# Another written order for the attention steps, the loads and the first expert's steps of an attention and mixture-of-experts kernel

## Chip, cores and metric

The kernel runs on one core of a Trainium2 chip. The metric is the device time of one execution in microseconds (us). The kernel before takes 1009.96 us, the median of three runs (1009.75 to 1012.1).

## What is computed

Two layers follow each other. The first is linear attention with exponential features, for 8 batches of 8 heads, 576 tokens and 64 values per head. The second takes its output as 4608 rows of 512 values and sends every row through all 8 experts, weighted by a routing matrix that eight rounds of row and column normalization make.

```
proj = einsum('bhsd,df->bhsf', x, w_phi)            # x is q or k
proj = proj - max(abs(proj), axis=-1)
phi  = concatenate([exp(proj), exp(-proj)], axis=-1)
kv = einsum('bhsf,bhsd->bhfd', phi_k, v);  z = sum(phi_k, axis=2)
attn = einsum('bhsf,bhfd->bhsd', phi_q, kv) / (einsum('bhsf,bhf->bhs', phi_q, z) + 1e-6)
...
P = exp(logits)                                     # logits = x @ w_gate
for _ in range(8): P /= P.sum(1); P /= P.sum(0); P *= N / E
for e in range(8): out += P[:, e:e+1] * (maximum(x @ w1[e], 0) @ w2[e])
```

## The kernel before, in words

**Records and planner.** The kernel's Python code does not issue instructions at once. Each operation is recorded with its engine, a cost in microseconds, the buffers and keys that it reads and writes, and a rank, which is its place in the recorded sequence (`Plan.op`). A scheduler (`Plan.schedule`) then walks through a modelled time: of all operations whose inputs are there and whose buffers can be had, it takes the one that can start first, and among equals the one recorded first. The instructions are written to each engine's queue in that order, and on the chip each engine works through its queue in order. So the recorded sequence is a priority, and the planner's costs decide the rest. Buffers are rings: an operation that needs a slot waits until an earlier user has given it back.

**The order string.** For the attention, its loads and the first expert, the recorded sequence is a string of 322 letters, `order` in line 1102 and after. Each letter records the next step of its kind. With head pairs counted j = 0 to 31 (batch j // 4, two heads each):

- `l` (14): loads the Q, K and V of half a batch (four heads). For batches 0 and 1 Q and K go through SyncE's queue (SP) in float32. From batch 2 on they go through GpSimd's queue (POOL, line 550) and are cast to bf16 on the way. V goes through SP (line 558).
- `e` (4): loads the 64 last tokens of each head, the "rests", of one or two batches (lines 600 to 607).
- `w` (8): loads a quarter of the first expert's w1 (the first four, line 527) or w2 (line 531), through POOL.
- `t` (12): from batch 2 on, a DMA transpose of a half batch's Q and K, issued by SP (line 567). There are two buffers of loaded Q and K (`qk`), and three of transposed ones (`qkT`).
- `r` (8): the features of a batch's rests (line 678 transposes, line 727 a small GpSimd step, lines 732 and 737 V scaled by GpSimd into `vrd`).
- `a` (32): a pair's K side. For batches 0 and 1 TensorE transposes Q and K (line 752) and VectorE and ScalarE copy them (lines 756, 760). Then come four K projections on TensorE (256 columns each), maxima on VectorE (line 614), exponentials on ScalarE (line 618), a sign change by GpSimd (line 808), the exponentials of the maxima `em`, and V scaled with them by GpSimd (lines 810 and 816).
- `q` (32): the four Q projections and their maxima. `p` (32): the Q features, two 512-column matmuls and four exponentials.
- `b` (32): the KV product of a pair, 18 small matmuls, and its copy by VectorE (line 892).
- `n`, `m` (32 each): the outputs of the pair's first and second head (line 905 on TensorE, lines 913, 918 and 919 on VectorE).
- `c` (32): the pair's output transposed into `xT`, by TensorE (line 934) and VectorE (line 937) in batches 0, 1, 2 and 7, by a DMA transpose (line 928) in batches 3 to 6.
- `g` (8): a batch's rests transposed (line 944), and its routing logits.
- `u` (24), `d` (20): up-projection (eight 512-column matmuls, `ps<-xT,w` under line 622) and down-projection (the same size, `ps<-w,hx`) of the first expert, for a quarter of a 512-token group. A `u` needs that group's `xT` and w1, a `d` the group's four `u` and w2.

Most matmuls of these steps are recorded by one helper and stand under line 622.

**Loads wait for the order too.** A load step carries `gates()`: it waits for the maxima of the last `q` and the last `a` that stand before it in the string. So a letter's place moves the load itself, not only its rank.

**After the string.** The rest of the first expert fills the time of the routing rounds, and then the other seven experts follow with a two-level fast multiplication, each with an order of its own written out. None of that changes.

Of the kernel before, what the change touches and what calls it, by code (L numbers as in the profile page):

```python
# [349 lines left out]
def kernel(  # L350
# [739 lines left out]
    def stage_g(b):  # L1090
# [9 lines left out]
             "c": lambda j: pair_c(j // 4, j % 4, xbs[j]), "g": stage_g,  # L1100
             "u": lambda i: up0(i // 4, i % 4), "d": lambda i: down0(i // 4, i % 4)}
    order = (
        "lraeaepqbwlqaqawwabwmqlltnrbppnwqbppmrmanbqaqmwwacmpnpbccpwbtcnmqnaqbclupunm"
        "taumquglcapalbcpnqqdcenmucugbblnapmrcqdutabnqpmunpbambccddnqplanmqmducpblttb"
        "augnaqlnrbdcampcadmqeutunqcppmdcaqtdqabpbbmlrqtdnpmuaqualbnagnacctbmqulupran"
        "tdpmtdqcmdnpdabdancpcabbqmpumqbcdgnappqunburqcbugmmnqdcdanumupqbnucmcpnmbddp"
        "bqmpncncubncmmgccg"
    )
    for i, n in enumerate(order):
        at[0] = i  # L1110
# [948 lines left out]
```

## Time and profile before

| quantity | value |
|---|---|
| median of the runs | 1009.96 us (1009.75 to 1012.1) |
| profiled execution, first to last instruction | 1008.8 us |
| TensorE busy (PE) | 994.0 us, 8376 matmuls |
| VectorE busy (DVE) | 898.6 us |
| ScalarE busy (ACT) | 812.8 us |
| GpSimd busy (POOL) | 447.6 us |
| attention on TensorE | until about 205 us, mixed with the first expert |
| granted TensorE clock | 1.000 |

The profile is of one execution. A row of the timeline gives the start and the length of an instruction (or of several alike in a row) in microseconds, then engine, line, operation, output tile, input tiles and shape; a bracket names the idle time ahead of it and who ended it. A matmul's row shows its whole passage: a stream of 512-column matmuls of 379 ns each starts a new one every 215 ns or so, so the step from start to start is what one costs. `SPq` and `POOLq` rows are the issuing of DMAs, not their transfer. A table of stretches gives each engine's busy time between two times.

### The profile page before, as it was taken

The numbers are of one execution on the slowest core, as the hardware profiler recorded it, in microseconds if no ns is written. First come the engines' busy times: TensorE is split into PE (matmuls) and PEld (weight loads), VectorE is DVE, ScalarE is ACT, GpSimd is POOL, SyncE is SP. The second block draws the span as 40 slices with busy tenths as digits, with TensorE's granted clock in tenths as the row PEclk, the third lists the DMA queues.
The fourth block names the chain that finished last, engine by engine and source line by source line (L and its number), as shares of the span: only waits on it lengthen the run. The fifth ranks groups of instructions, "written<-read, shape, count | busy, mean of one in ns | idle before, by whom it ended". The sixth has DMA issues, their size and how long they took to land.

```text
span 1008.8 us, 23309 instructions
## 1 busy us (share of the span) xinstructions
PE 994.0 (99%) x8376; PEld 727.7 (72%) x8376; DVE 898.6 (89%) x1999; ACT 812.8 (81%) x1930; POOL 447.6 (44%) x514
## 2 busy tenths in 40 slices
PE   7899999999999999999999999999999999999998
PEld 5666666644566877777777877787778777787775
DVE  7999998987888998899989898989889988989886
ACT  7999999845979788878878788777887888778874
POOL 5778674400133344434444444444443444344443
PEclk9999999999999999999999999999999999999999
DMA  9999999181136423282327133632246222724653
GB/s 249 183 202 183 157 153 144 38 170 56 53 121 143 147 97 98 84 184 96 109 98 170 44 100 131 130 127 98 97 117 177 97 98 84 147 79 142 208 174 126
DMA packets 129748, 128.86 MB, mean 128 GB/s; under 512 B 55776, under 2 KB 98272, under 8 KB 129632
## 3 DMA queue, kind: packets, MB, share of 16 engines
q1 hardware_dynamic: 97680, 103.33, 36.3%
q0 software_dynamic: 31648, 23.86, 16.9%
q8 instruction: 65, 1.06, 0.5%
q14 instruction: 51, 0.42, 0.2%
q10 hardware_dynamic: 304, 0.20, 0.1%
HBM read 122.50 MB, written 19.53 MB: 141 GB/s over the span
## 4 chain that ended last, share of the span: by engine, by line
PE 92%; DVE 3%; ACT 2%; DMA 2%; issue 1%; POOL 0%; DVEq 0%
PE ps L1466 41%; PE ps L1475 20%; PE ps L622 17%; PE ps L1607 11%; PE ps L905 2%; DMA xi6t<-X 1%; DMA xi<-X 1%; PE ps L752 1%; ACT q L618 0%; DVE m L614 0%; ACT k L618 0%; DVE wx L614 0%; DVE X L1240 0%; DMA acc<-in_k_dram 0%; DVE hs L1676 0%
## 5 line engine op out<-in xcount | busy, mean ns | idle before, releaser
L1875 POOL TENSOR_TENSOR acc<-acc,hx 128x512 f32<-128x512 f32 x186 | 236.1, 1276 | 404.7 <-ACT hx L1872 135.0
L1466 PEld LDWEIGHTS <-hs 128*128 128x128 bf16 x1984 | 194.1, 98 | 46.4 <-issue 0.2
L1872 ACT ACTIVATE hx<-ps,P 128x256 f32<-128x256 f32 x372 | 158.9, 483 | 53.4 <-PE ps L1466 52.0
L1860 DVE SCALAR_TENSOR_TENSOR acc<-ps,P,acc 128x256 f32<-128x256 f32 x372 | 162.2, 478 | 30.2 <-PE ps L1466 28.2
L1475 PE MATMUL ps<-xT,T 128*128 128x512 bf16 x608 | 171.0, 379 | 0.0
L1466 PEld LDWEIGHTS <-hx 128*128 128x128 bf16 x1488 | 145.6, 98 | 24.9
L1466 PE MATMUL ps<-hx,hs 128*128 128x256 bf16 x992 | 144.3, 273 | 0.0
L1676 DVE CUSTOM_DVE_ANT_0 hs<-ps,U 128x512 bf16<-128x512 f32 x192 | 124.7, 684 | 11.3 <-PE ps L1475 6.6
L1607 PE MATMUL ps<-xT 128*128 128x256 bf16 x576 | 125.4, 272 | 0.0
L1475 PEld LDWEIGHTS <-T 128*128 128x128 bf16 x672 | 65.8, 98 | 40.6
L1682 ACT ACTIVATE hs<-ps 128x512 bf16<-128x512 f32 x96 | 55.9, 598 | 41.7 <-PE ps L1475 40.2
L1466 PE MATMUL ps<-wx,hs 128*128 128x256 bf16 x560 | 78.4, 273 | 0.0
L622 PE MATMUL ps<-w,hx 128*128 128x512 bf16 x288 | 73.0, 379 | 0.0
L622 PE MATMUL ps<-xT,w 128*128 128x512 bf16 x288 | 72.9, 379 | 0.0
L1466 PE MATMUL ps<-wx,hx 128*128 128x256 bf16 x496 | 72.3, 273 | 0.0
L1676 DVE CUSTOM_DVE_ANT_0 hs<-ps,X 128x512 bf16<-128x512 f32 x96 | 65.1, 684 | 7.8 <-PE ps L1607 6.9
L1466 PE MATMUL ps<-hx 128*128 128x256 bf16 x496 | 71.2, 273 | 0.0
L1607 PEld LDWEIGHTS <-xT 128*128 128x128 bf16 x576 | 56.3, 98 | 17.5
L1466 PE MATMUL ps<-w,hx 128*128 128x256 bf16 x432 | 62.2, 273 | 0.0
L614 DVE TENSOR_REDUCE m<-ps 128x4 f32<-128x512 f32 x88 | 58.8, 680 | 3.7 <-PE ps L622 1.9
L1672 ACT COPY X<-ps 128x512 f32<-128x512 f32 x96 | 58.6, 610 | 2.5 <-DVE ps L1650 2.5
L1466 PE MATMUL ps<-w,hs 128*128 128x256 bf16 x432 | 60.2, 273 | 0.0
(174 smaller groups left out, 2256.0 us busy)
## 6 DMA issues: line engine op xcount, KB each, us to landing
xT<-xi SPq DMA_DIRECT2D x48, 448.0 KB, 4.6
xT<-xd SPq DMA_DIRECT2D x72, 256.0 KB, 4.0
wx<-in_moe_w_dram POOLq DMA_DIRECT2D x8, 1024.0 KB, 11.2
v_m<-in_v_dram SPq DMA_DIRECT2D x15, 512.0 KB, 5.2
out_dram<-acc SPq DMA_DIRECT2D x14, 512.0 KB, 3.0
w<-in_moe_w_dram POOLq DMA_DIRECT2D x6, 1024.0 KB, 11.0
xT<-xp SPq DMA_DIRECT2D x24, 256.0 KB, 2.8
qk<-in_k_dram POOLq DMA_DIRECT2D x12, 256.0 KB, 5.4
```

The costliest lines, as they stand in the source:

```text
L614: dve(el, lambda: nc.vector.tensor_reduce(out=dst(), in_=src(), axis=AX.X, op=ALU.max, apply_absolute_value=True), r, w)
L622: nc.tensor.matmul(out_, lhsT=lhsT, rhs=rhs, start=start, stop=stop)
L905: pe(65, lambda j=j: nc.tensor.matmul(pn()[:, j * D1:j * D1 + D1], lhsT=s["T"][x]()[:, j % 2, 2 * h + j // 2, :] if j < 4 else r["T"][x]() ...
L1466: pe(256, lambda i=i, k=k, z=z: nc.tensor.matmul(bank()[:, 256 * i:256 * i + 256], lhsT=lhs(k, i), rhs=rhs(k), start=first and z, stop=k = ...
L1475: pe(512, lambda k=k: nc.tensor.matmul(bank().rearrange("p (a b) -> p a b", a=2), lhsT=lhs(k), rhs=rhs(k), start=first and k == 0, stop=k ...
L1607: pe(256, lambda: nc.tensor.matmul(halves_of(bank[q], n)(), lhsT=lhs(), rhs=t()[:, rhs, :], start=start, stop=True, skip_group_check=True) ...
L1672: act(512, lambda: nc.scalar.copy(out=flat(to[q])(), in_=bank[q]()), [bank[q]], [(to[q], 0), (to[q], 1)])
L1676: dve(515, lambda: nc.vector._custom_dve(ADD_SAT, out=out_(q, i, j), in0=bank[q]().rearrange("p (a b) -> p a b", a=2), in1=to[q](), s0=3.0 ...
L1682: act(512, lambda: nc.scalar.activation(out=out_(q, i, j), in_=bank[q]().rearrange("p (a b) -> p a b", a=2), func=ACT.Relu, bias=0.0, scal ...
L1860: dve(320, lambda n=n, ts=ts: nc.vector.scalar_tensor_tensor(out=acc[g][:, ts, 256 * j:256 * j + 256], in0=bank()[:, 256 * n:256 * n + 256 ...
L1872: act(370, lambda n=n: nc.scalar.activation(out=u()[:, n, :], in_=bank()[:, 256 * n:256 * n + 256], func=ACT.Copy, bias=0.0, scale=P[:, 4 ...
L1875: pool(695, lambda: nc.gpsimd.tensor_tensor(out=acc[g][:, 2 * i:2 * i + 2, 256 * j:256 * j + 256], in0=acc[g][:, 2 * i:2 * i + 2, 256 * j: ...
```

## The change

Only the string `order` is different. It has the same letters the same number of times, and the code that records each step is the same, so the built programs hold the same matmuls, vector operations and DMAs; how many extra instructions only wait for a semaphore differs by 0 to 11 an engine.

```diff
     order = (
-        "lraeaepqbwlqaqawwabwmqlltnrbppnwqbppmrmanbqaqmwwacmpnpbccpwbtcnmqnaqbclupunm"
-        "taumquglcapalbcpnqqdcenmucugbblnapmrcqdutabnqpmunpbambccddnqplanmqmducpblttb"
-        "augnaqlnrbdcampcadmqeutunqcppmdcaqtdqabpbbmlrqtdnpmuaqualbnagnacctbmqulupran"
-        "tdpmtdqcmdnpdabdancpcabbqmpumqbcdgnappqunburqcbugmmnqdcdanumupqbnucmcpnmbddp"
-        "bqmpncncubncmmgccg"
+        "rlaeqpaaqebwwqmbwlapnmqrnabpccnmpbqwaclwwaplptaqbwaqbmarnqcqmnpblumnuwclunlb"
+        "mbpptcacnautmgqbtcpuenqummbpcnuacqlramddpnbqqatdbtapnumcrcapnlqadbqaqptbmlba"
+        "adgpcdmlptumnubqcuqbenmaquapdngmpqbccdqulbqrtalpmmnndbdptgmbcacrmnqundnqcpbm"
+        "bulucdgcapncduqanpqmdbmnpdbtntamcupmducbrqcunaqaguqapnbppbncdmaddcnpbqmubqcn"
+        "mbmupunpmmncccdgcg"
     )
```

Some places of letters in the string, counted from 0:

| step | before | after |
|---|---|---|
| first four `w` (w1) | 9, 15, 16, 19 | 11, 12, 16, 35 |
| last four `w` (w2) | 31, 46, 47, 58 | 39, 40, 49, 69 |
| first four `l` | 0, 10, 22, 23 | 1, 17, 38, 43 |
| first three `t` | 24, 60, 76 | 45, 80, 87 |
| first `u`, first `d` | 71, 95 | 65, 114 |
| first four `c` | 49, 55, 56, 61 | 28, 29, 37, 58 |

## Prediction

> **What bounds the kernel now.** I read the page's busy rows and forty slices first, then the table of stretches, then single rows of the timeline where the early stretches lose time.
>
> ```profile
> span 1008.8 us, 23309 instructions
> ...
> PE 994.0 (99%) x8376; PEld 727.7 (72%) x8376; DVE 898.6 (89%) x1999; ACT 812.8 (81%) x1930; POOL 447.6 (44%) x514
> ...
> PE   7899999999999999999999999999999999999998
> ...
> PEclk9999999999999999999999999999999999999999
> DMA  9999999181136423282327133632246222724653
> ```
>
> TensorE is the bound: busy 994.0 of 1008.8 us, so 14.8 us at most can be won by any order of the same instructions. Only its first two slices and its last are not full. The DMA row is full in just the first seven slices.
>
> ```profile
> 0.00:25.00 25.00, 18.52 (x157) 12.62 (x157) 19.63 (x38) 19.42 (x47) 13.42 (x27) 1.00 1.08 248
> 25.00:50.00 25.00, 22.12 (x257) 15.43 (x256) 24.48 (x56) 24.89 (x65) 18.96 (x35) 1.00 1.30 185
> 50.00:75.00 25.00, 24.63 (x330) 17.33 (x328) 24.29 (x60) 24.20 (x60) 17.87 (x28) 1.00 1.12 200
> 75.00:205.00 130.00, 130.00 (x1523) 84.89 (x1522) 118.88 (x278) 122.13 (x298) 83.63 (x133) 1.00 0.90 132
> ...
> 0.00:52.00 52.00, 42.36 (x431) 29.20 (x432) 46.11 (x98) 46.31 (x116) 34.36 (x63) 1.00 1.19 218
> 52.00:75.00 23.00, 22.91 (x309) 16.18 (x309) 22.29 (x56) 22.20 (x55) 15.88 (x26) 1.00 1.12 195
> ```
>
> The first figure after each stretch is its length, then follow PE, PEld, DVE, ACT and POOL busy, the granted clock, the DMA share and GB/s. TensorE idles 6.48 + 2.88 + 0.37 = 9.7 us in the first 75 us and not at all from 75 to 205 us. In the first 52 us it idles 9.6. There VectorE and ScalarE carry the attention, 24.5 and 24.9 us busy of 25, while TensorE has nothing of the first expert to fill in with: the first up-projection starts at 45.48 us. From there on it fills every gap, and 0.1 us is lost from 52 to 75 us. So the kernel is an early stage of about 45 us that VectorE and ScalarE set, then 960 us of TensorE.
>
> ```profile
> 45.48 0.38 PE L622 MATMUL ps<-xT,w 128*128 128x512 bf16 x1
> ...
> 50.10 0.38 PE L934 MATMUL ps<-ident,xb 128*128 128x128 bf16 x4
> 50.32 1.03 PE L622 MATMUL ps<-xT,w 128*128 128x512 bf16 x4
> 51.18 0.28 PE L905 MATMUL ps<-wx 128*128 128x65 bf16 x4
> 51.30 0.20 PE L905 MATMUL ps<-wx,qr 128*128 128x65 bf16 x1
> ...
> 52.00 0.60 PE L622 MATMUL ps<-wphi,qkT 128*128 128x256 bf16 x4 [0.28 <-DVE m L614]
> ```
>
> From one row's start to the next, a 512-column matmul takes (51.18 - 50.32) / 4 = 0.215 us, a 128-column transpose 0.055, a 65-column one 0.03. The last row is the first projections of batch 2, whose inputs come through a DMA transpose.
>
> **The change part by part.** The built programs hold the same 8376 matmuls and 1999 VectorE operations. On TensorE the two orders are the same from matmul 2513 on (258 us in the trace), on VectorE and ScalarE from 252 and 259 us on. All that can move lies ahead of that, and since 75 to 205 us is full, most of it ahead of 75 us.
>
> *Until the first up-projection.* In the new order 371 matmuls stand ahead of it instead of 349 (a KV product and two output groups more, four transposes and two feature matmuls less). VectorE must have done two more maxima, one more KV eviction and one normalization less before it.
>
> ```profile
> 10.28 1.89 DVE L614 TENSOR_REDUCE m<-ps 128x4 f32<-128x512 f32 x3 [0.52 <-PE ps L622]
> ...
> 22.23 0.43 DVE L892 CAST kv<-ps 128x260 bf16<-128x260 f32 x1
> ...
> 24.12 0.49 DVE L919 TENSOR_TENSOR xb<-ps,rec 128x320 bf16<-128x320 f32 x1
> ```
>
> That is 2 x 0.63 + 0.43 - 0.49 = +1.2 us on the engine that sets this stage, against +0.26 us of matmuls moved ahead. What is won against it: the new order lets VectorE take the first pair's four maxima in one row while the second pair's Q and K are still on their way, where it now waits 0.52 us for TensorE (row above). I give that 0 to 0.7 us. This part alone is 0.2 to 1.2 us lost at the first up-projection, but it is not additive with the next one: both are ready-times of the same TensorE queue.
>
> *The first DMA transpose of batch 2.* This is the term that I let decide. GpSimd's queue issues the loads that feed it, in written order with its arithmetic. Now:
>
> ```profile
> 33.59 1.04 POOL L732 TENSOR_TENSOR vrd<-v_r,em_r 64x512 bf16<-64x512 f32 x1 [2.64 <-ACT em_r L618]
> 34.60 0.23 POOL L808 TENSOR_SCALAR m<-m 128x8 f32<-128x8 f32 x1
> 34.78 0.61 POOL L527 DMA_DIRECT2D w<-in_moe_w_dram  x1
> 35.40 0.76 POOL L550 DMA_DIRECT2D qk<-in_k_dram  x1
> 36.17 1.92 POOL L810 TENSOR_TENSOR v<-v_m,em 128x1024 bf16<-128x1024 f32 x1
> ...
> 38.16 0.82 POOL L550 DMA_DIRECT2D qk<-in_q_dram  x1
> ...
> 40.45 0.25 POOL L737 CAST vrd<-em_r 64x8 bf16<-64x8 f32 x1
> ...
> 41.89 0.77 POOL L531 DMA_DIRECT2D w<-in_moe_w_dram  x1
> ...
> 35.21 0.35 ACT L618 ACTIVATE em<-m 128x16 f32<-128x16 f32 x1
> ```
>
> In the new order the second batch's rest (L732, L737, twice), the V scaling of pair 4 (L808, L810, L816), the fourth part of w1, the K load, then the whole V scaling of pair 5 stand ahead of that Q load. ScalarE's em_r comes 1.5 us of work earlier, so L732 starts at 32.1; the four rest operations take 1.01 + (41.89 - 40.45) = 2.45 and end at 34.55. The exponentials of pair 4 (em) have the same work ahead as now (ready 35.3), so L810 runs 35.3 to 37.1, with L816 until 37.3; w1's part 0.6, L808 0.2 and the K load 0.8 bring it to 38.9, the second L810 to 40.8, L816 to 41.0. The Q load issues at 41.0 instead of 38.16, behind arithmetic it did not stand behind before.
>
> ```profile
> 42.56 8.41 SPq L567 DMA_TRANSPOSE qkT<-qk  x2
> ...
> DMA to landing us min/median/max: 8.6/8.6/8.6
> ...
> DMA to landing us min/median/max: 4.3/7.3/8.6
> ...
> qk<-in_q_dram POOLq DMA_DIRECT2D x1, 256.0 KB, 4.3
> ...
> qk<-in_q_dram POOLq DMA_DIRECT2D x1, 256.0 KB, 5.7
> ```
>
> The transpose is issued 42.56 - 38.16 = 4.4 us after the Q load and lands 8.6 us later (first landing row), at 51.2, just ahead of the projection at 52.00; the seven such transposes from 30 to 110 us take 4.3, 7.3 and 8.6 us (least, median, most). In the new order it is issued at 41.0 + 4.4 = 45.4 and lands at 45.4 + 7.3 = 52.7. I take the median, because the 8.6 is of a transpose that shared its time with two more Q and K loads and the next transpose, which now come later. Bounds: 45.4 + 4.3 = 49.7, and 41.0 + 5.7 + 8.6 = 55.3.
>
> TensorE gets there with 430 matmuls ahead instead of 431: five small ones more, two of 512 and four of 128 columns fewer, 0.15 - 0.43 - 0.22 = -0.5 us. With the idle time of now it would arrive at 51.5. So it waits 1.2 us, and it is in order: the eight projections stand in the middle of a KV product, with up-projections behind them that could have run. The bounds give a stall from nothing to 3.8 us. After it, 52 to 75 us now loses only 0.1 us, so there is nothing to give the stall back.
>
> *The next transposes and the first expert's weights.*
>
> ```profile
> 63.03 1.04 PE L622 MATMUL ps<-wphi,qkT 128*128 128x256 bf16 x8
> ...
> 63.62 1.94 POOL L810 TENSOR_TENSOR v<-v_m,em 128x1024 bf16<-128x1024 f32 x1
> ...
> w<-in_moe_w_dram POOLq DMA_DIRECT2D x1, 256.0 KB, 6.0
> ```
>
> The second transpose will be needed by projections with as much matmul work ahead as those at 63.03, so at 64.2 with the stall. Its Q load stands behind the V scaling of pair 6; by the same steps I put its issue at 50.5 to 51.5, the landing at 50.5 + 4.4 + 7.3 = 62.2 to 51.5 + 5.7 + 7.3 = 64.5. It costs 0 to 0.3 us; I take nothing. Of the weights, w1's last part is issued at 37.3 instead of 34.78 and used after 46 us. w2's last part moves most: behind the V scaling of pair 9, which runs at 63.62 now and about as late then, so it is issued near 65 and lands near 71. Its first down-projection, with some 735 matmuls ahead (744 start in the first 75 us now), comes near 76. The up-projections written ahead of it cover the delay; if that cover were 5 us thinner, it would stall by what is missing. I take 0.
>
> **Sum.** +1.2 us on a span of 1008.8. The profiled execution's span is 1.2 us below the median of the runs, 1009.96 (1009.75 to 1012.1), and I leave that difference: 1009.96 + 1.2 = 1011.2 us.
>
> A rule against the stall: the Trainium skill, DMA: Bandwidth & Descriptors, section Latency and other measured facts, gives DMA transposes 261 GB/s and a DMA a fixed cost of about 2 us. By it the 512 KB would take an estimated 4.0 us, land at 49.4 and cost nothing. The trace's own 4.3 to 8.6 us speak against it wherever the queues are shared.
>
> **The rivals.** *Nothing waits.* If the transpose takes 4.3 us, as the fastest did, it lands at 49.7, ahead of TensorE. What is left is VectorE's stage: between 0.7 won and 1.2 lost, so 1009.3 to 1011.2, about 1010.0. For it: fewer transfers run beside the transpose. Against it: the median. By the page's rule this is the outcome.
>
> *A chain of late transposes, slower.* Only two Q/K buffers exist, so GpSimd's next K load waits for the transpose two before it, and everything behind in its queue, V scaling included, waits too. The point at which it decides: transposes of 8.6 us after Q loads of 5.7. Then the first costs 3.8 us, the second (51.5 + 5.7 + 8.6 = 65.8 against 63.0 + 3.8) nothing more, but the third and fifth, with pair 9 and later behind the waiting load, about 1 us each: 3.8 to 5.8 us, 1013.8 to 1015.8. For it: the first transpose now does take 8.6. Against it: a half batch needs some 11 us of TensorE, more than one transpose, so it catches up. The Trainium skill, TensorE: Matmul & The Clock Gate, section HAM oscillation, adds that idle gaps over about 3.4 us halve the clock, which would make this rival dearer; the quoted stretches show a clock of 1.00 throughout, and no gap that long, so no run here shows it.
>
> *A gain.* If the early 0.7 us carries through and 52 to 75 us loses nothing, TensorE's idle time falls by 1 to 2 us: 1008.5. More than 3 us would need the first up-projection three microseconds earlier, against 1.2 us more VectorE work ahead of it.
>
> *No effect at all*, the recorded order undone by the scheduler, is excluded: each engine's built order differs from its 10th to 25th instruction on.
>
> **How the numbers follow.** A measurement of this kernel can tell about 0.3%, 3 us, from no change. Forecast (a stall of some 1 us, 1010.2 to 1012.5): 0.47. Nothing waits: 0.25. Chain, or another wait of its size between 75 and 250 us that I did not see: 0.22. Gain: 0.06. Only the chain crosses +3 us, and 0.03 of the forecast with it, less 0.03 of the chain's near end: slower 0.22. Faster by over 3 us takes half of the gain, 0.03; same 0.75. The range leaves out the chain's far half and the gain's: 1008.5 to 1015.0.
>
> **What would show it.** Right: the first DMA transpose issued near 45 us and landing near 53; the projections after it starting 0.5 to 1.5 us later than 52.00 with a wait named; TensorE's idle time in 0 to 52 us at about 10.5, and 75 to 205 us full again. The step on the first up-projection is right if it starts between 46 and 47 us. Wrong: the transpose in place before 51 us, TensorE idle in 75 to 205 us, or more than 1 us of change behind 260 us, where the order is the same.

## The result and the profile after

The new order takes 1025.21 us (median of five executions, 1021.68 to 1028.65), against 1009.96 (1009.52 to 1012.1) for the order before: 1.0149 times as long, with a 95% interval of 1.013 to 1.0168. The forecast of 1011.2 and its range to 1015.0 were far too low. The profiled execution has a span of 1022.1 us, 13.3 more than before.

The page of the profile after, its busy rows, slices and the start of its chain of waits:

```profile
span 1022.1 us, 23297 instructions
...
PE 994.7 (97%) x8376; PEld 728.0 (71%) x8376; DVE 898.8 (88%) x1999; ACT 814.5 (80%) x1930; POOL 448.2 (44%) x514
...
PE   7879999999999999999999999999999999999998
...
PEclk9989999999999999999999999999999999999999
DMA  9999699343233813371336322552237222724653
...
PE 88%; DMA 6%; ACT 2%; DVE 2%; issue 1%; SPq 1%; POOL 0%; DVEq 0%; ACTq 0%
```

The work is the same (PE 994.7 us, 8376 matmuls), the third slice is not full any more, and in the same slice the granted clock drops. The stretches of after show where else TensorE idles:

```profile
25.00:50.00 25.00, 21.17 (x264) 15.13 (x265) 24.81 (x59) 24.72 (x65) 19.49 (x34) 1.00 1.10 193
50.00:75.00 25.00, 19.01 (x225) 12.95 (x224) 17.09 (x41) 17.73 (x42) 15.40 (x25) 0.86 0.89 127
75.00:100.00 25.00, 23.25 (x260) 15.22 (x258) 22.77 (x52) 23.20 (x58) 18.29 (x30) 1.00 1.43 191
...
125.00:150.00 25.00, 23.15 (x275) 14.95 (x273) 21.80 (x52) 21.80 (x55) 16.71 (x28) 1.00 0.94 145
150.00:175.00 25.00, 23.22 (x270) 15.12 (x269) 21.65 (x50) 23.02 (x56) 18.49 (x29) 1.00 1.27 191
...
54.10:60.90 6.80, 3.50 (x27) 2.62 (x28) 2.25 (x4) 2.44 (x6) 1.20 (x2) 0.50 1.13 124
75.00:205.00 130.00, 124.41 (x1419) 80.36 (x1417) 114.37 (x260) 120.35 (x294) 80.29 (x130) 1.00 0.94 146
```

Two things are new. From 54.1 to 60.9 us the granted clock is 0.50; TensorE is busy for 3.50 us of that, of which half, 1.75 us, is by estimate what the clock costs. And 75 to 205 us, where the order before has TensorE busy for 130.00 of 130.00 us, now has 124.41. From 205 us on the two orders run alike: TensorE idles for 5.1 us there before and for 5.4 after. The timeline of after gives TensorE's waits, in brackets, with the first up-projection ahead of them:

```profile
45.73 0.59 PE L622 MATMUL ps<-xT,w 128*128 128x512 bf16 x2 [1.42 <-DVE m L614]
...
57.40 1.89 PE L622 MATMUL ps<-wphi,qkT 128*128 128x256 bf16 x8 [5.99 <-DMA qkT<-qk]
...
84.53 0.28 PE L622 MATMUL ps<-wphi,qkT 128*128 128x256 bf16 x1 [1.60 <-DMA qkT<-qk]
...
101.29 0.28 PE L622 MATMUL ps<-wphi,qkT 128*128 128x256 bf16 x1 [0.21 <-DMA qkT<-qk]
...
125.54 0.27 PE L622 MATMUL ps<-wphi,qkT 128*128 128x256 bf16 x1
...
143.00 0.28 PE L622 MATMUL ps<-wphi,qkT 128*128 128x256 bf16 x1 [1.72 <-DMA qkT<-qk]
...
158.78 0.61 PE L622 MATMUL ps<-wphi,rT 128*128 128x256 bf16 x4 [1.78 <-DMA rT<-qk_r]
```

The eight projections at 57.40 take 1.89 us, where eight took 1.04 at 63.03 us before: that is the half clock in a row. The waits on transposes are 5.99 + 1.60 + 0.21 + 1.72 + 1.78 = 11.3 us, the half clock 1.75, the later first up-projection 45.73 - 45.48 = 0.25. Together 13.3 us, which is the difference of the spans. That they meet so exactly is in part luck: as a whole TensorE's idle time grew by 27.4 - 14.8 = 12.6 us and its busy time by 0.7, and small waits on other engines, which differ too, are not in the list.

The five executions have spans of 1019.9, 1022.1, 1023.4, 1025.5 and 1026.9 us, at mean granted clocks of 0.997, 0.996, 0.995, 0.993 and 0.993. The longer an execution, the lower its clock, which fits more time at half clock; only the one of 1022.1 us was traced.

### The profile page after: what moved, and what is told of

Its sections match the earlier page's. It is cut to its first block, busy times and chain, and to the rows that moved or that the text cites. A ratio compares the mean times of both kernels' runs of the same rounds, so it can differ in the third digit from the quotient of the medians.

```text
span 1022.1 us, 23297 instructions
## 1 busy us (share of the span) xinstructions
PE 994.7 (97%) x8376; PEld 728.0 (71%) x8376; DVE 898.8 (88%) x1999; ACT 814.5 (80%) x1930; POOL 448.2 (44%) x514
## 4 chain that ended last, share of the span: by engine, by line
PE 88%; DMA 6%; ACT 2%; DVE 2%; issue 1%; SPq 1%; POOL 0%; DVEq 0%; ACTq 0%
PE ps L1466 40%; PE ps L1475 19%; PE ps L622 16%; PE ps L1607 10%; DMA qkT<-qk 3%; PE ps L905 1%; DMA w<-in_moe_w_dram 1%; DMA xi6t<-X 1%; DMA rT<-qk_r 1%; DMA acc<-in_q_dram 0%; ACT k L618 0%; ACT q L618 0%; DVE m L614 0%; ACT kr L618 0%; DVE X L1240 0%
## 5 line engine op out<-in xcount | busy, mean ns | idle before, releaser
L1872 ACT ACTIVATE hx<-ps,P 128x256 f32<-128x256 f32 x372 | 159.2, 483 | 53.1 <-PE ps L1466 50.5
L1860 DVE SCALAR_TENSOR_TENSOR acc<-ps,P,acc 128x256 f32<-128x256 f32 x372 | 162.1, 477 | 30.3 <-PE ps L1466 28.3
L614 DVE TENSOR_REDUCE m<-ps 128x4 f32<-128x512 f32 x88 | 58.6, 680 | 5.7 <-PE ps L622 5.2
L1466 PE MATMUL ps<-w,hx 128*128 128x256 bf16 x432 | 62.2, 273 | 0.0
```

The lines of the kernel that those rows point to most:

```text
L614: dve(el, lambda: nc.vector.tensor_reduce(out=dst(), in_=src(), axis=AX.X, op=ALU.max, apply_absolute_value=True), r, w)
L1466: pe(256, lambda i=i, k=k, z=z: nc.tensor.matmul(bank()[:, 256 * i:256 * i + 256], lhsT=lhs(k, i), rhs=rhs(k), start=first and z, stop=k = ...
L1860: dve(320, lambda n=n, ts=ts: nc.vector.scalar_tensor_tensor(out=acc[g][:, ts, 256 * j:256 * j + 256], in0=bank()[:, 256 * n:256 * n + 256 ...
L1872: act(370, lambda n=n: nc.scalar.activation(out=u()[:, n, :], in_=bank()[:, 256 * n:256 * n + 256], func=ACT.Copy, bias=0.0, scale=P[:, 4 ...
```

## The experiments

**The theories.** A, from the trace above: a late Q load, a long transpose, TensorE in order behind it, and a clock that halves after the long wait. B, formed after the first four kernels: every half batch has lost the lead of its load over its use, and TensorE, once it comes earlier, meets the next late transpose. Rivals: the arithmetic's new order is itself slower; the transfers are slow because of what runs beside them; VectorE's early stage is late. C came last: the new order sits between two limits. A difference counts against the order before, run beside each kernel (medians of 1009.97 to 1011.22 us).

### Waits on transposes, taken away and nothing else moved

Three kernels keep every queue as it is and change only what TensorE reads.

```diff
+            if b >= 2:      # a_free, b_free;  a_free_first: b == 2 and pr < 2
+                return W[0][0]()[:, x, 128 * o:128 * (o + n)]
             return t["T"]()[:, x, o:o + n, :].rearrange("p a b -> p (a b)")
```

(The first two read w1 in the rests' matmuls too.)

> The new order with the same instructions in the same places on every queue, loads and DMA transposes included, but TensorE's projections and feature matmuls of batches 2 to 7 read the first expert's w1 (there since 32 us) in place of the transposed Q, K and rests, so nothing that TensorE does waits for a DMA transpose. (The numbers that come out are then not the attention's.) Theory B (all of the loss is TensorE waiting in order for late transposes, with the half clock that such a wait brings): the six named waits (11.3 us) and the half clock go, span 1022.1 - 13 = 1009, within 1 us of the order before. Rival (the new order of the arithmetic is itself slower, and without the transposes TensorE waits for VectorE and ScalarE instead): span 1012 to 1020. If the arithmetic's order is better than before, under 1007.5.

> The control: the order before with the same replacement of operands. Its transposes land ahead of their use (TensorE has no named wait on them), so both theories expect the span of before, 1008.8 within 0.5 us. A lower time by more than that would mean that waits on transposes are hidden in before's issue time too.

> The new order with that replacement for the first half of batch 2 alone: the first wait (6.0 us at 51 us) and its half clock (1.8 us) are taken away and all the rest, each queue and each load, stays where it is. If the waits add up, the span falls by 7.8 us to 1014.3. Theory B with feedback (TensorE that comes earlier meets the later transposes earlier, and those are paced by loads that hang on VectorE's and GpSimd's progress): the first 75 us gain 7 to 8 us, the waits near 84, 143 and 159 us grow, by up to 1 to 3 us each and with a half clock where one passes some 3.4 us; span 1016 to 1021.

The new order without these waits takes 1012.36 us (ratio 1.0021, 1.0009 to 1.0034), the old one 1010.7 (1.0004, 0.9994 to 1.0013). So 12.85 of the 15.25 us are TensorE's waits on DMA transposes with the clock that goes with them, and about 2 us are the order of the arithmetic. TensorE's projections of the first half in the new order, freed:

```profile
51.96 1.03 PE L622 MATMUL ps<-wphi,w 128*128 128x256 bf16 x8
```

They run at 51.96 instead of 57.40 and at full clock, while the transpose that they no longer need still lands at 48.27 + 6.8 = 55.1 us. So the cost is shown to be these waits and their clock; why the transposes are late is not yet shown by it.

With the first half alone freed the time is 1018.93 (1.0089, 1.0068 to 1.0109): 6.3 us less, where the first wait and its half clock are 7.8 together. The interval is some 2 us wide to either side, so the time alone does not tell 6.3 from 7.8; the trace does. TensorE comes to the third half earlier, and waits there longer, with a half clock behind it; the trace of that kernel:

```profile
78.77 0.61 PE L622 MATMUL ps<-wphi,qkT 128*128 128x256 bf16 x4 [2.79 <-DMA qkT<-qk]
```

```profile
76.40:79.80 3.40, 1.03 (x7) 0.70 (x8) 0.87 (x2) 0.65 (x3) 0.84 (x2) 1.00 1.47 200
79.80:83.30 3.50, 3.50 (x15) 1.49 (x13) 2.45 (x5) 1.71 (x6) 3.50 (x8) 0.51 0.98 179
```

A wait that is taken away comes back in part at a later transpose, which is theory B's feedback.

### The clock by itself

```diff
+                def warm(on):
+                    for _ in range(52 if on else 0):
+                        mm(pp[1][0]()[:, 0:256], wphi2f[:, 0:128], wphi2f, True, True)
```

> The new order with 52 extra matmuls of 256 columns (features weights times themselves, about 0.109 us each, 5.7 us in all, into the PSUM bank that the next projection overwrites) put ahead of the blocked projection of batch 2; all else is as it was, on every queue. It separates the idle time from the clock. Theory A: the extra work fills 51.4 to 57.1 us, the projection starts at 57.4 as before, the granted clock stays at full speed, and the span falls by what the half clock cost, 1.7 to 1.9 us, to about 1020.3. Rival (the slow rows after the wait come from the projections themselves, or from waiting for VectorE, and the clock costs nothing): span stays at 1022.

Measured: 1025.43 us (1.0155, 1.0126 to 1.0183), as without the fill; the interval is too wide to show 1.75 us. Locally the half clock goes, in its trace:

```profile
50.59 5.84 PE L622 MATMUL ps<-wphi 128*128 128x256 bf16 x52
...
56.26 1.04 PE L622 MATMUL ps<-wphi,qkT 128*128 128x256 bf16 x8
...
144.18 0.61 PE L622 MATMUL ps<-wphi,qkT 128*128 128x256 bf16 x2 [5.20 <-DMA qkT<-qk]
```

The projections after the filled gap run at full clock (1.04 us, 0.85 less than in the new order). They start behind the fill, 3.1 us after their transpose landed in this execution (46.90 + 6.25 = 53.15 us). But TensorE then came earlier to the eighth half, whose transpose took 8.1 us in this execution (5.9 in the one above), waited 5.20 us and lost the clock there, from 140.9 to 147.7 us. So 0.85 us of the clock's price is shown, in these eight projections; the rest of the 1.75 is worked out from the granted clock, and nothing of it is seen at the end. The first transpose took 6.3 us here, with the same queues for which the profiled execution of the new order shows 9.6: such a transfer varies by 3 us from execution to execution.

### The first half's load earlier; other loads out of its way

```diff
-        "rlaeqpaaqebwwqmbwlapnmqrnabpccnmpbqwaclwwaplptaqbwaqbmarnqcqmnpblumnuwclunlb"
+        "rlaeqpaaqebwwqmbwlapnmqrlnabpccnmpbqwacwwaplptaqbwaqbmarnqcqmnpblumnuwclunlb"
+        "rlaeqpaaqebwwqmbwlapnmqrnabpccnmpbqwaclaplptaqbwaqbmarnqcqmnwwpblumnuwclunlb"
```

The first new line, with the third `l` earlier, is a_early_l; the second, with two `w` later, a_late_w2.

> The new order with one letter moved: the third l (Q, K and V of the first half of batch 2) stands at place 24 instead of 38, so GpSimd issues that K and Q load ahead of the V scaling of pairs 3 to 5, Q near 33 us instead of 41.36. Theory A (a late Q load, then a long transpose, then an in-order TensorE, then a clock that halves after the long wait): the transpose is issued near 38 to 39 and lands at 45 to 49, ahead of TensorE (51.4); the 6.0 us wait and the stretch at half clock (about 1.8 us) both go, so the span falls from 1022.1 by 6 + 1.8 to about 1014.3, or to 1012.5 if the third transpose's wait of 1.8 us near 84 us goes too; the two waits of 1.9 us near 143 and 159 us stay, since their letters are where they were. Rival 1 (the later waits are an echo of the first one): those go as well, span about 1009. Rival 2 (the early stage of VectorE and ScalarE is what is late, and the wait on the transpose only shows it): TensorE waits about as long for something else, span 1020 to 1022.

The early load gave 1021.24 us (1.0103, 1.0086 to 1.012). The transpose was issued at 37.73 us and landed after 4.9; wait and half clock at 51 us were gone. Of the 7.8 us, 4.0 arrived at the end. So VectorE's stage was not the limit, and part of what was won is lost again (the letter also moved some of the arithmetic behind it in the planned queues). In its trace the rest's transpose now costs 3.11 us instead of 1.78, and a half clock (155.8 to 159.2 us) that was not there:

```profile
155.53 0.80 PE L622 MATMUL ps<-wphi,rT 128*128 128x256 bf16 x4 [3.11 <-DMA rT<-qk_r]
```

> The new order with the first two w2 letters moved from places 39 and 40 to 62, so that these two 512 KB loads no longer follow the Q load at once on GpSimd's queue. Rival (contention: the Q load took 6.2 us instead of 4.4 and the transpose 9.6 instead of 7.3 because the w2 parts run beside them): Q load about 4.4 and transpose about 7.3 us again, landing near 53, TensorE waits about 1.5 us instead of 6.0, no half clock, span about 1016. Theory A without contention (the sizes are what a transpose beside V loads takes): Q load about 6, transpose about 9.6, wait about 6 us, span about 1022. Half of each: a wait of 3 to 4 us, which also shows whether the clock halves after a wait of that length.

1032.25 us (1.0223, 1.0198 to 1.0247), slower. The transpose took 6.4 us and TensorE's first wait was 3.38, again with a stretch at half clock (55.2 to 58.6 us). That does not show contention, since 6.3 us occurred beside the w2 loads too. And the planner's order behind the attention changed with the string: 350 to 450 us has TensorE busy for 96.35 us, where the new order has 100.00. A moved letter moves more than its own step, which spoils this experiment as a test.

### The planner told that transposes are slow

```diff
-            270: (500, 48), 90: (340, 75), 148: (265, 30), 160: (540, 50)}
+            270: (500, 48), 90: (340, 75), 148: (90, 30), 160: (540, 50)}
```

> The new order with only the planner's cost of DMA transposes changed (90 GB/s instead of 265, 512 KB in 5.8 us instead of 2.0). The planner then writes the projections of batch 2 behind 141 more matmuls (571 instead of 430), up-projections above all, and the later transposed tiles' users behind more work as well. Theory A with in-order TensorE (the loss is not the late transpose by itself but that TensorE's written order puts its user too early): TensorE arrives near 61.4 us, the transpose is there (57.3), no wait and no half clock, and the later waits shrink too; span 1009 to 1012. Rival 1 (the chain of loads and transposes through two buffers is too slow as a whole): the waits only move to later transposes, span 1015 to 1020. Rival 2 (VectorE, whose work now comes later, takes over as the bound): span 1012 to 1016 with idle TensorE that names VectorE.

All theories missed: 1052.66 us (1.0413, 1.0396 to 1.043). No wait on a transpose of Q, K or rests is among TensorE's named waits; it waits in small pieces for VectorE and ScalarE, as the table of waits between 40 and 200 us shows:

```profile
PE ps L622 <- DVE m L614: 4.8, 11, 1.4
PE ps L622 <- ACT k L618: 2.5, 6, 0.7
PE ps L622 <- ACT kr L618: 1.9, 1, 1.9
```

75 to 205 us has TensorE busy for 116.73 of 130 us. That explains only part of the 27 us over the new order: TensorE's busy time rose as well, from 994.7 to 1008.5 us. That up-projections written ahead of the late projections are then missing as filling later is my guess, not tested. Putting the use later in this way is no cure.

### Only the load letters moved

```diff
-        "lraeaepqbwlqaqawwabwmqlltnrbppnwqbppmrmanbqaqmwwacmpnpbccpwbtcnmqnaqbclupunm"
+        "lraeaepqbwlqaqawwabwmqnrbppnwqbppmrmaltnbqlaqmwwacmpnpbccpwbtcnmqnaqbcupunma"
...
-        "rlaeqpaaqebwwqmbwlapnmqrnabpccnmpbqwaclwwaplptaqbwaqbmarnqcqmnpblumnuwclunlb"
+        "rlaeqpaaqebwwqmbwlapnmqrnallbpccnmpbqwacwwapptaqbwaqbmarnqlcqmnpbumnuwclunlb"
```

The first lines of the strings of b_loads (the order before, loads later) and a_loads (the new order, loads earlier); further `l` move in the lines behind. Their variants with freed operands add the edit of a_free.

> The mirror: the order before with the same eight l put behind as many K and Q steps as in the new order (two t follow, since a transpose cannot stand ahead of its load); all else as before. Theory B: the first transpose of batch 2 is issued near 47 us and lands at 53 to 57, TensorE gets there near 52 and waits 1 to 5 us, with half a clock if it is over 3.4; the eighth transpose's load stands behind 14 us more of VectorE's work than before and may cost another 0 to 2; span 1010 to 1016. Rival (the late loads are harmless in the old order, and what costs is how the new one puts the arithmetic): span within 1 us of 1008.8.

> The order before with the eight l put later (as in the kernel of 1024 us), and the projections and feature matmuls of batches 2 to 7 reading w1 in place of the transposed tiles (the numbers are then not the attention's); the queues are the same as without that replacement. Theory B (late loads cost because TensorE waits in order for the transposes behind them, and for no other reason): 1010 to 1013 us, so that the whole 14 us are waits on transposes with their half clock. Rival (loads later in the string also move the planner's arithmetic and make GpSimd or VectorE late): over 1016.

> The new order with only load letters moved: the eight l of batches 2 to 7 that stand behind more K and Q steps than in the order before (the first two, and those of the sixth to tenth half among others) are put back behind as many K and Q steps as there. Theory B (every half batch has lost the lead of its load over its use, so that the waits of TensorE come from the loads' places all along the attention, and a wait that is cured in one place alone is met again at the next late transpose, as the kernel with one letter moved showed): the waits of 6.0 us near 51 us and 1.9 us near 143 us go with the half clock, those near 84 and 159 us may stay, since VectorE's work ahead of their loads hardly changes; span 1009 to 1014. Rival (the chain is bound by something that the loads' places do not set, VectorE's work or SyncE's queue of transposes): the waits come back further on, span 1017 to 1021.

> The new order with the eight l put earlier (as in the kernel of 1032 us) and the same replacement. There the trace shows 3.65 us of TensorE lost between 350 and 450 us that the new order does not lose, from another planned order behind the attention, and a wait of 4.4 us on a rest's transpose. Theory B: the waits on transposes go, the 3.65 us stay: 1014 to 1017 us. Rival (moving the loads earlier spoils the order of the arithmetic in the attention): 1020 or more.

Later loads in the old order give 1023.99 us (1.0151, 1.0123 to 1.0179), all of the slowdown of the new one and more than either theory gave. But with the waits on transposes taken away it is still 1017.03: half of the 14 us are waits on transposes. The rest is not told apart: the planner's arithmetic moved as well, and the loads stand differently among GpSimd's work. Earlier loads in the new order give 1032.44, and 1028.58 without the waits. So the load letters are not the whole of it, and my theory B missed there. Moving letters can't tell loads and arithmetic apart; the next kernels do.

### The finished queues permuted: only loads and transposes move

```diff
-        done = self.schedule()
+        done = self.hoist(self.schedule(), 8.0, (568, 585, 622, 704))
```

The four lines are the Q and K loads, their transposes, and the same two of the rests. `hoist` moves these DMAs forward in the planned sequence, `sink` back, each as far as its needs, its buffer and the given time allow. TensorE, VectorE, ScalarE and GpSimd's arithmetic keep their order.

> The mirror in the order before: the same loads and transposes moved back by at most 4 us of the planner's time each, never past their first use; all arithmetic queues unchanged. Transposes there land 0.8 us (the first half of batch 2) to 14 us ahead of their use, three or four of them by less than 4 us. Theory B: waits on transposes of 3 to 7 us at the first, and of 1 to 5 us at two or three more, with half clocks: 1018 to 1030 us. Rival (before has a cover that the traces do not show, or the arithmetic sets all): under 1013.

> The kernel before with the moved-back loads and transposes, and TensorE reading w1 in place of the transposed tiles of batches 2 to 7 (the numbers are then not the attention's). Theory B: 1010 to 1011.5, as with the order before, since nothing waits for a transpose and no arithmetic was moved. Rival (later loads hurt by holding up GpSimd's arithmetic): 1014 or more.

b_sink takes 1019.69 us (1.0087, 1.0058 to 1.0116), b_sink_free 1013.78 (1.0037, 1.0024 to 1.005). The first is near the low end of theory B's range; the second is 2.3 us above theory B's and 0.2 below its rival's 1014. Loads and transposes that are up to 4 us later thus cost 9.5 us in the old order, 5.9 of them as waits on transposes. In b_sink's trace (its line 640 is line 622 above):

```profile
55.40 1.15 PE L640 MATMUL ps<-wphi,qkT 128*128 128x256 bf16 x8 [3.43 <-DMA qkT<-qk]
81.05 0.28 PE L640 MATMUL ps<-wphi,qkT 128*128 128x256 bf16 x1 [1.93 <-DMA qkT<-qk]
96.73 0.27 PE L640 MATMUL ps<-vrd,kr 128*128 128x130 bf16 x2 [1.88 <-POOL vrd L755]
```

The last row shows the other part, which theory B left out and the rival had named: a load that stands differently among GpSimd's work delays V scaled by GpSimd. Here the K load at 92.42 us (0.80 to issue) and the Q load at 94.35 (0.82) stand ahead of and between the two halves of that scaling, which ends at 96.68.

> The new order, planned as it is; then, in the finished queues, every K and Q load on GpSimd's queue and every DMA transpose of loaded Q, K and rests on SyncE's queue is moved forward by at most 8 us of the planner's time, never past what it needs nor past the last use of its buffer. The queues of TensorE, VectorE and ScalarE and the order of GpSimd's arithmetic are unchanged. Theory B (the loads stand too late against their use, and that alone is the loss): the six waits shrink to 0 to 2 us in all, no half clock, 1012 to 1016 us (1012.4 is what the new order takes when nothing waits for a transpose). Rival (the transfers themselves are the limit: loads issued earlier take longer, or wait for their two buffers and hold up the V scaling behind them): 1020 or more.

> The same with at most 16 us. Theory B: no better than with 8 us, 1012 to 1016, since 8 us cover the longest wait (6.0). Rival (loads that stand too early wait in GpSimd's queue for one of the two Q/K buffers, with the V scaling behind them): 1018 or more, with TensorE waiting for V scaled by GpSimd (line 816).

> Two buffers, loads and transposes up to 4 us earlier instead of 8. Theory C: GpSimd's wait for a buffer and TensorE's wait for scaled V get smaller by some 4 us, part of the waits on transposes comes back; between the two limits 1018 to 1025 us. Rival (the waits of the eight-microsecond kernel have nothing to do with how early the loads stand): 1025 or more.

> As the kernel whose loads stand up to 8 us earlier, and with a third buffer for loaded Q and K for the third, sixth and ninth half of batches 2 to 7 (in an accumulator that the first expert does not use before 180 us); the queues hold the same instructions. Theory C (the new order leaves no room between two limits: with late loads TensorE waits for transposes, with early ones the load waits for its buffer in GpSimd's queue and TensorE waits for the V scaling behind it): the 5.8 us wait of GpSimd at 65 us and TensorE's 7.4 us go, waits on transposes stay away, 1012 to 1017 us. Rival (earlier loads cost by the crowd of transfers, or because each load on GpSimd's queue delays V scaling by its issue): 1020 or more.

> The new order's finished queues with the loads and transposes of only the first, third, seventh and eighth half of batches 2 to 7 moved forward, by at most 5 us of the planner's time: those whose Q load is issued only 10 to 12 us ahead of their projections in the new order (14 to 30 in the old). Sixteen lines of GpSimd's queue and five of SyncE's differ, all arithmetic stands where it was. Theory C: the buffers are free there, so nothing waits on GpSimd; the waits on transposes near 51, 84 and 143 us (9.5 us) and the half clock go, the wait on a rest's transpose near 159 us stays with 1.8 to 3; 1012 to 1017 us. Rival (any load that comes earlier costs as much by holding up V scaling as it gains): 1020 or more.

| loads in the new order | time | ratio (interval) | TensorE waits for |
|---|---|---|---|
| as written | 1025.21 | 1.0149 (1.013 to 1.0168) | transposes of Q, K and rests 11.3 us |
| up to 4 us earlier | 1034.91 | 1.0226 (1.0205 to 1.0246) | transposes of Q and K 5.7, of outputs 3.7, ScalarE 4.3, POOL 4.3 |
| up to 8 us | 1026.0 | 1.0153 (1.0138 to 1.0168) | POOL 13.0, no transpose of Q, K or rests |
| up to 16 us | 1037.87 | 1.0273 (1.0256 to 1.029) | POOL 14.0, ScalarE 3.3, transposes of outputs 2.1 |
| up to 8 us, third buffer | 1021.68 | 1.0109 (1.0086 to 1.0132) | POOL 7.4, no transpose of Q, K or rests |
| four halves, up to 5 us | 1024.41 | 1.0134 (1.0097 to 1.017) | rests' transposes 3.7, Q and K 2.2 |

None of the five came out where theory B or C had it: they stand on the side of the rivals, the third buffer 4.7 us above its 1017. With 8 us the waits on transposes of Q, K and rests are all gone, and the time is the same, because the wait has moved. GpSimd's queue and TensorE in that kernel:

```profile
65.35 0.82 POOL L568 DMA_DIRECT2D qk<-in_k_dram  x1 [5.76 <-DMA qkT<-qk]
66.19 1.92 POOL L828 TENSOR_TENSOR wx<-v_m,wx 128x1024 bf16<-128x1024 f32 x1
...
69.17 1.04 PE L640 MATMUL ps<-wx 128*128 128x65 bf16 x16 [7.41 <-POOL wx L834]
```

The K load of the fourth half stands in the queue for 5.76 us, until a transpose frees one of the two Q/K buffers; the V scaling behind it waits too, and TensorE 7.41 us for that, with a half clock from 63.8 to 74.0 us. The third buffer takes this wait away, and 4.3 us of time: that part of theory C is shown. What is left there are waits on GpSimd of up to 1.9 us. Why 4 us earlier costs more than 8 is open; its trace has two transposes longer than any other here, 13.2 us (issued at 44.08) and 14.5 (at 70.98), and behind the second of them GpSimd's next K load waits 8.25 us for its buffer.

With only the four halves of small lead moved, the first wait is 1.58 us instead of 5.99, the one at 143 us is gone, and the rest's transpose costs more:

```profile
53.12 1.05 PE L648 MATMUL ps<-wphi,qkT 128*128 128x256 bf16 x8 [1.58 <-DMA qkT<-qk]
...
156.74 1.03 PE L648 MATMUL ps<-wphi,rT 128*128 128x256 bf16 x4 [3.01 <-DMA rT<-qk_r]
```

Its span is 1022.2 us. The granted clock is 0.50 from 155.9 to 162.7 us. Again what was won ahead was lost at the next late transpose.

## Why the prediction was wrong, point by point

**The bound and the first up-projection.** TensorE is the bound, as said. The first up-projection started 0.25 us later, within the 0.2 to 1.2 that the sum allowed, though at 45.73 us and not between 46 and 47.

**The deciding term was the right place, and a fifth of what it cost.** The queue arithmetic held: the Q load was issued at 41.36 us (41.0 forecast), TensorE arrived at 57.40 - 5.99 = 51.4 (51.5). What failed were the two transfers. After's rows on GpSimd's and SyncE's queues, and their landing times:

```profile
41.36 0.83 POOL L550 DMA_DIRECT2D qk<-in_q_dram  x1
...
47.71 3.11 SPq L567 DMA_TRANSPOSE qkT<-qk  x1
```

```profile
qk<-in_q_dram POOLq DMA_DIRECT2D x1, 256.0 KB, 6.2
...
qkT<-qk SPq DMA_TRANSPOSE x1, 9.6
```

From the Q load's issue to the transpose's are 6.35 us, not 4.4, and the transpose took 9.6, not 7.3. That is 1.95 + 2.3 us; with the Q load 0.36 later and TensorE 0.1 earlier it makes the 5.99 of the 1.2. Both lie above my bounds (5.7 and 8.6). My reason for the median, that less would run beside this transpose, was not borne out: two w2 loads followed the Q load at once, and the second half's K and Q loads were issued at 48.03 and 50.89 us, while it ran. How much of the 9.6 us comes from them is not shown; a_fill has 6.3 with the same queues. The bounds were too tight for the trace of before itself, where Q loads take 4.3 to 8.0 us and the eighth half's transpose, behind the 30 to 110 us that I had looked at, 10.3:

```profile
114.55 5.10 SPq L567 DMA_TRANSPOSE qkT<-qk  x1
...
qkT<-qk SPq DMA_TRANSPOSE x1, 10.3
```

In all these kernels Q and K transposes take 4.2 to 14.5 us.

**The second transpose and the weights.** Neither costs anything, as forecast, but for the second transpose that is luck. It was issued at 62.21 us and landed at 68.12, not between 62.2 and 64.5; TensorE came for it only at 70.06 instead of 64.2, because it had lost so much at the first.

**The clock.** I left the half clock out because the trace of before showed no long gap and a clock of 1.00 throughout. Neither is quite so: TensorE waits 3.99 us for its first input, the clock records begin only at 9.7 us (the stretches count what lies ahead as 1.00), and there four 256-column projections take 0.81 us (6.11 to 6.92), where four at 11.52 us take 0.44. My upper bound of the stall, 3.8 us, should have carried the clock's price. The half clock cost an estimated 1.75 us here. The Trainium skill's rule (TensorE: Matmul & The Clock Gate, section HAM oscillation, that idle gaps above about 3.4 us throttle the array) agrees with this trace for the 5.99 us wait. Where they differ the measurement decides: in the kernel with the first half freed a wait of 2.79 us was enough, and in a_loads_free one of 3.11 us (125.19 to 128.30) passed at a clock of 1.00.

**The step that failed by the most: "75 to 205 us is full".** Beyond the 1.2 us forecast, the profiled execution lost 4.8 us at the first transpose, 1.75 by the clock and 5.3 at waits between 80 and 160 us, for which the prediction has nothing. I worked out two transposes of twelve and let a full stretch of the trace of before stand for the rest. A full stretch tells that nothing was late there, not by how much it was not late. I should have set the lead of each load beside what load and transpose take. From the issue of the Q load to TensorE's arrival at that half's first projection (its wait taken off):

| half, batch 2 on | before: issue, arrival, lead | after: issue, arrival, lead | wait after |
|---|---|---|---|
| first | 38.16, 52.00, 13.8 | 41.36, 51.4, 10.0 | 5.99 |
| second | 39.71, 63.03, 23.3 | 50.89, 70.06, 19.2 | 0 |
| third | 60.19, 74.56, 14.4 | 70.96, 82.9, 12.0 | 1.60 |
| fourth | 62.86, 86.46, 23.6 | 73.22, 95.11, 21.9 | 0 |
| fifth | 77.54, 98.02, 20.5 | 85.86, 101.1, 15.2 | 0.21 |
| sixth | 81.79, 109.85, 28.1 | 92.22, 115.87, 23.7 | 0 |
| seventh | 94.88, 119.12, 24.2 | 115.64, 125.54, 9.9 | 0 |
| eighth | 98.20, 128.47, 30.3 | 130.79, 141.3, 10.5 | 1.72 |
| ninth | 114.35, 144.44, 30.1 | 139.03, 154.34, 15.3 | 0 |

Each of these nine leads shrank, by 1.7 us (the fourth) to 19.8 (the eighth). Where TensorE waits, the lead fell below what load and transpose together took in after: 16.0 us for the first half, 13.5 for the third, 15.4 for the fifth and 12.2 for the eighth. At the seventh only a quick pair, 9.4 us, saved the wait; at the second, fourth, sixth and ninth the transposes landed 1.4 to 8.7 us ahead of their use. A lead is not yet a margin, though: in before the eighth half has a lead of 30.3 us, yet its transpose, issued late and long, lands only 3.6 us ahead of its use. From landing to use the margins of the nine in before are 0.9, 9.4, 2.5, 9.0, 6.5, 14.4, 11.4, 3.6 and 14.4 us. All that could be read before the change was run, and the leads in the new order estimated from the queues as for the first half.

**The rivals.** "A chain of late transposes, slower" had the right sign and the late transposes, but not for its reason: it makes loads wait for one of the two Q/K buffers, and in after GpSimd does so once before 180 us, for 1.36 us (the K load at 85.04). That chain shows in the kernels with earlier loads. Its price, 1013.8 to 1015.8, was wrong by its own terms: the first wait (3.8 at most), no half clock, 1 us each for the third and fifth, nothing for the eighth and for the rest. "Nothing waits" is refuted. The 261 GB/s of the Trainium skill (DMA: Bandwidth & Descriptors, section Latency and other measured facts), by which the prediction estimated 4.0 us for this transpose, stand against 9.6 measured. "1 us of change behind 260 us" did not occur.

**What stays open.** That the waits on transposes are 12.85 of the 15.25 us is shown. That they come from loads which stand too late is shown only in part, and the spread of the transposes themselves has its share: later loads slow the old order, but earlier ones don't speed up the new one beyond 1021.2 us, since GpSimd's queue, two buffers and the rests' transposes take over. Which order of the arithmetic leaves room for all of them was not tried; no version beat the order before. Of the 2 us of the arithmetic itself I have no breakdown.

## What to carry to other kernels

When an order changes and transfers feed an in-order engine, list for every transfer its issue, its landing and its use, in the profile of before, and work out the lead and the margin of each in the new order; a stretch without idle time says nothing about the margin. Take a transfer's bound from all transfers of its kind, over several executions, and price a wait of 3 us or more on TensorE with the half clock as well. A wait that is cured may only be met again at the next late transfer: predict the end from the last stretch in which something is late, and test causes by changing operands or finished queues, not by moving letters that a planner reads.

## What the runs showed of the hardware

No single length of wait decides on the half clock in these kernels. In the attention, behind the first 20 us, each wait of TensorE of 3.28 us or more had a stretch at a granted clock of 0.50 during it or within 3.5 us of its end (3.28 in a_hoist16, 3.38 in a_late_w2, 3.43 in b_sink, up to 8.62). Of those from 1.9 to 3.2 us some had one (1.91 in a_slowT, 1.94 in a_late_w2, 2.79 in a_free_first, 3.01 in a_hoist_some, 3.11 in a_early_l) and some none (2.03 and 3.11 in a_loads_free, 2.76 in b_loads). And it does not need one long gap. In b_loads the stretch from 49.8 to 53.2 us has a granted clock of 0.50, though no wait ahead of it in that stretch of the timeline is above 0.70 us; the 3.4 us ahead of it have TensorE busy for 2.23:

```profile
46.40:49.80 3.40, 2.23 (x26) 1.41 (x25) 3.37 (x9) 3.40 (x9) 3.25 (x7) 0.99 1.35 188
49.80:53.20 3.40, 3.18 (x8) 1.20 (x9) 2.01 (x5) 2.11 (x5) 3.31 (x5) 0.50 1.15 179
```

Nor is the busy share of such a stretch the rule: b_loads_free has the same queues and the same four waits there (0.70, 0.19, 0.34 and 0.51 us), and its eight matmuls that follow take 2.10 us at a clock of 1.00. What decides between the two is open. All stretches at half clock in the attention of these kernels last 3.4, 6.8 or 10.2 us.

A 512 KB DMA transpose of the same place in the queues took 6.3, 6.8, 8.3 and 9.6 us in four executions whose queues were alike (a_fill, a_free, a_free_first and the new order), and 8.6 and 6.3 us in two of the order before (before and b_free).
